# Attention scores masked in the accumulator bank, probabilities transposed before they are split, in a fused attention and two-layer MLP kernel

## The chip, the cores and the metric

One core of a Trainium2 chip runs the kernel. The metric is the device time of one execution in microseconds (us): the median of three runs, 1299.41 us (1298.48 to 1299.56) before the change. The engines are TensorE (PE; PEld for its weight loads), VectorE (DVE), ScalarE (ACT), GpSimd (POOL) and SyncE (SP, which issues the DMAs).

## The reference

The inputs are q, k and v of 4 batches, 8 heads, 768 positions and head size 64, in float32. Each query sees the first 4 keys (the sinks) and the last 128 keys up to itself; then come two dense layers over 3072 tokens.

```python
scores = scale * np.matmul(q, k.transpose(0, 1, 3, 2))
keep = is_sink | in_window
scores = np.where(keep, scores, -1000000000.0)
scores = scores - np.max(scores, axis=-1, keepdims=True)
a = np.exp(scores)
a = a / (np.sum(a, axis=-1, keepdims=True) + 1e-09)
x = np.matmul(a, v)                  # 3072 x 512 after the heads are joined
h = np.maximum(x @ moe_w_in, 0.0);  x = h * h @ moe_w_out         # 512 -> 2048 -> 512
h = x @ moe2_w_in;  out = (h - np.tanh(h)) @ moe2_w_out           # 512 -> 2048 -> 512
```

## The kernel before

**Precision.** Most matmuls take float32r operands (a reduced float32 that TensorE takes at full rate). To keep float32 accuracy an operand is split in two: `xh` is the value rounded to float32r, `xl` the rest. A product is then three matmuls (high by high, low by high, high by low). The first 16 jobs of attention, the *plain* ones, use unsplit float32 instead.

**Attention.** A *job* is one head of one half sequence (384 queries); 64 jobs make 8 *blocks* of 384 tokens. Jobs 0 to 15 are plain (`plain`), jobs 16 to 63 are split (`job`, `scores`, `values`): 48 of them. A job has three *units* of 128 queries. A unit multiplies its queries with 260 key columns: the 128 keys before its own, 4 sink keys, its own 128 keys (lines 323 and 324, the high and the low part of the keys; one result bank `S` for all units). Then ACT or DVE copies 132 columns of `S` to the tile `cb` (line 332 and the copies before it, recorded as line 257 on ACT and 259 on DVE), DVE overwrites with the earlier keys where the mask `up` says so (line 332, `copy_predicated`: a query has 128 keys in its window, and every column holds either an earlier or an own key), DVE adds the mask `m` and takes the row minimum of the negated scores (`least`, line 393, a custom instruction followed by a read of its accumulator `nm`), and ACT takes the exponential and the sum (line 336). After three units the sums are inverted (340, 341) and `cb` is multiplied by them (349). The first unit of a sequence's first half has no earlier keys: its two parts are copied one by one, without line 332.

**Transposition.** The 384 probability columns of a job are split into the float32r tiles `a` (high: a cast of 384 columns, on ACT or DVE; low: a subtraction on DVE, recorded as line 267). TensorE transposes both into bank `T` in two groups: four transpositions for the first two units (line 368), then two for the third and one for the sinks' tile `ask` (370). Each group is copied out to `xe` (or `pt`), and POOL selects from `xe` the own and the earlier keys into `pt` (line 382). Lines 413 to 418 multiply the values with `pt` into bank `O`; DVE joins the parts (429, 431) and splits the result into `xh`, `xl`, the input of the first layer.

**Layers.** `step1` makes one of 16 hidden slices of the first layer for a block: 12 matmuls into bank `ph` (line 579), relu (609 on ACT, 611 on DVE), square (615, 617), split into `gh` and `gl`, and 12 matmuls into four `acc` banks (593). `step2` is the second layer with 512 columns (579, 595). Weights arrive as 64-bit words and are decoded and split by `w_split` (lines 552 to 565).

**What sets the order.** Every operation is entered with its reads, its writes, a priority (a due time in planned microseconds) and its assumed duration per engine. `Order.solve` plays the program through with these durations: at each point an engine takes the most urgent operation that is ready, and operations that can run on more than one engine go where they would end first. The instructions are then issued in that order, each engine's queue in order. A wrong assumed duration therefore changes no result, but makes an engine wait in front of an instruction that came too early in its queue.

Of the kernel before, what the change touches and what calls it, by code (L numbers as in the profile page):

```python
# [33 lines left out]
KW = (3 * P + 2 * SK, 4 * P + 3 * SK)  # L34
# [28 lines left out]
class Op:  # L63
    __slots__ = ("engs", "prio", "emit", "left", "out", "ready", "start", "eng", "end")
# [13 lines left out]
class Order:  # L78
# [11 lines left out]
    NEAR = 60.0  # L90

# [3 lines left out]
    def add(self, engs, prio, reads, writes, emit):  # L95
        op = Op()
        op.engs, op.prio, op.emit, op.left, op.out, op.ready, op.eng = engs, prio, emit, 0, [], {}, None
        deps = set()
        for k in reads:
            if k in self.writer:  # L100
                deps.add(self.writer[k])
            self.readers.setdefault(k, []).append(op)
        for k in writes:
            if k in self.writer:
                deps.add(self.writer[k])
            deps.update(self.readers.pop(k, ()))
            self.writer[k] = op
        deps.discard(op)
        for d in deps:
            d.out.append(op)  # L110
        op.left = len(deps)
        self.ops.append(op)
# [3 lines left out]

    def solve(self):
        free = {e: self.AHEAD.get(e, 0.0) for op in self.ops for e in op.engs}
        avail, pend = {e: [] for e in free}, {e: [] for e in free}
        rank = {id(op): i for i, op in enumerate(self.ops)}  # L120
# [3 lines left out]
        def offer(op):  # L124
            for e in op.engs:
                heapq.heappush(pend[e], (op.ready.get(e, 0.0), rank[id(op)], op))

        for op in self.ops:
# [6 lines left out]
        def cost(op, e, now):  # L135
            c = op.engs[e]
            if e == "T":
                n = int((self.FIRST + now) // self.TICK)
                t = c[0] if tick.get(n - 1, 0.0) >= 0.375 * self.TICK else 2.0 * c[0]
                tick[n] = tick.get(n, 0.0) + c[0]  # L140
                return t, t + c[1] - c[0]
            return c[0], c[1]

# [4 lines left out]
        while len(done) < n:  # L148
            e = min(free, key=lambda g: free[g])
            now = free[e]  # L150
# [4 lines left out]
            best, held, skipped = None, None, []  # L155
            while avail[e]:
# [5 lines left out]
                if all(max(free[g], op.ready.get(g, 0.0), port if op.engs[g][2] else 0.0) + queue(g, item) + op.engs[g][1] >= at + op.engs[e][1]  # L162
                       for g in op.engs if g != e):
                    if at <= now + self.NEAR:
                        if held is None or now + op.engs[e][0] <= held[0] + self.NEAR:
                            best = op
                            break
                    elif held is None:
                        held = (at, item)
                        continue  # L170
                skipped.append(item)
            if held is not None:
                if best is None:
                    best = held[1][2]
                else:
                    skipped.append(held[1])
            for item in skipped:
                heapq.heappush(avail[e], item)
            if best is None:
# [4 lines left out]
                continue  # L184
            at = begin(best, e, now)
            occ, took = cost(best, e, at)
# [34 lines left out]
def c_copy(n, psum=False):  # L221
    return {"A": c_act(n, psum), "V": c_one(n, psum)}


def c_pool(n):
    return C(2.35 * n + 110, 2.35 * n + 115, True)
# [12 lines left out]
class Fast:  # L239
# [11 lines left out]
    def copy(self, prio, reads, writes, get, n, psum=False):  # L251
# [8 lines left out]
        self.o.add(c_copy(n, psum), prio, reads, writes, emit)  # L260
# [19 lines left out]
    def job(self, j, due):  # L280
# [24 lines left out]
        self.copy(d - 8, [("rv", r)], [("vh", k2)], lambda: (t["vv", k2][:, :nv, vh], vals()), nv * D)  # L305
# [4 lines left out]
    def scores(self, j, half, due):  # L310
# [4 lines left out]
        cb, nm, ss, rs, a, ask, xe, pt = ("cb", k2), ("nm", k2), ("ss", k2), ("rs", k2), ("a", 0), ("ask", k2), ("xe", 0), ("pt", 0)  # L315
        cbs = [(*cb, i) for i in range(3)]
        for i in range(3):
            d, ks = due[i], cbs[i:i + 1]
            col = 132 * i if half else 132 * max(i - 1, 0)

            def qk(e, i=i, col=col):
# [3 lines left out]
            o.add({"T": c_mm(260, 260)}, d - 14, [("qh", k2), ("ql", k2), ("kh", k2), ("kl", k2)], [sb], qk)  # L325
            if i < i0:
                self.copy(d - 13, [sb], ks, lambda i=i: (t[cb][:, i, :SK], bank[sb][:, 128:132]), SK, True)
                self.copy(d - 13, [sb], ks, lambda i=i: (t[cb][:, i, SK:], bank[sb][:, :128]), P, True)
            else:
# [4 lines left out]
            self.least(d - 11, ks[0], [(*nm, i)], lambda i=i: t[cb][:, i, :], lambda i=i: t[nm][:, i:i + 1], half, i, -0.125)  # L334
# [20 lines left out]
        self.copy(d - 8.9, cbs, [(*ask, 0)], lambda: (sinks(0), t[cb][:, :, :SK]), 3 * SK)  # L355
# [5 lines left out]
        def slots(i, n, s):  # L361
            return t[pt].rearrange("p (n t) q -> p n t q", t=2)[:, 2 * i:2 * (i + n), s, :]
        for u, n in ((0, 2), (2, 1)):
# [704 lines left out]
```

## Time and profile before

The profiled execution took 1298.54 us, of which the span from first to last instruction is 1296.8 us; the median of the runs is 1299.41 us.

| engine | busy us | share of span |
|---|---|---|
| PE | 1263.2 | 97% |
| DVE | 1054.7 | 81% |
| ACT | 674.6 | 52% |
| POOL | 184.7 | 14% |

The program has four stages, which overlap at their ends: plain attention and decoding of the first weights (to about 190 us); split attention beside the first layer (190 to 670); the end of the first layer beside the decoding of the second layer's weights (670 to 838); the second layer alone. In the rows below a stretch's line gives the length of the stretch, then per engine the busy time and the number of instructions, PE's granted clock (1.00 is 2.4 GHz), the DMA share and GB/s. A timeline line gives start, length, engine, line, operation and its tiles; matmuls overlap, so the time that one costs is the distance from its start to the next start. A line of instruction groups gives the count, busy time and mean ns of one, then the engine's idle time before them and who ended it. A line of waits gives total, times and longest.

### The profile page before, as it was taken

To read this page: it belongs to the slowest core of one execution; us is meant where nothing else is said; L and a number is where in the kernel's file an instruction comes from. 1 tells how busy PE (TensorE), PEld (TensorE's weight loads), DVE (VectorE), ACT (ScalarE), POOL (GpSimd) and SP (SyncE) were. 2 spreads that over 40 slices of the span, in tenths; PEclk is the share of its full clock that TensorE was granted. 3 is DMA by queue.
4 is the path that set the end of the run, shared out by engine and by line. 5 is a ranking of instruction groups with operands and counts; after the bars stand their busy time and mean duration, and the time that the engine had idled before them with its cause. 6 is when DMAs were issued, how large, how long until landed. Compare 5 with 4: busy or idle time off the path is not lost.

```text
span 1296.8 us, 19460 instructions
## 1 busy us (share of the span) xinstructions
PE 1263.2 (97%) x6696; PEld 1115.6 (86%) x6696; DVE 1054.7 (81%) x2550; ACT 674.6 (52%) x1723; POOL 184.7 (14%) x332
## 2 busy tenths in 40 slices
PE   8999999999999999999999999999999999999997
PEld 5789999999999999999999978888888888888886
DVE  6899998877878777878768999977877877877775
ACT  5776776655666556566545566433432433432332
POOL 1221343132112222112311200000000000000000
PEclk9999999999999999999999999999999999999999
DMA  6974112211212112122118830100100200000001
GB/s 214 320 260 153 45 56 77 83 54 44 80 45 84 58 46 75 53 60 83 29 34 286 280 107 1 33 33 1 63 3 1 66 1 1 33 1 1 33 1 35
DMA packets 41724, 95.00 MB, mean 73 GB/s; under 512 B 4752, under 2 KB 18576, under 8 KB 41616
## 3 DMA queue, kind: packets, MB, share of 16 engines
q1 hardware_dynamic: 41472, 93.27, 22.4%
q8 instruction: 54, 0.88, 0.3%
q10 hardware_dynamic: 144, 0.40, 0.1%
q14 instruction: 54, 0.44, 0.1%
HBM read 79.50 MB, written 14.16 MB: 72 GB/s over the span
## 4 chain that ended last, share of the span: by engine, by line
PE 75%; DVE 16%; ACT 4%; issue 3%; DMA 1%; POOL 1%; SPq 0%; DVEq 0%; ACTq 0%; POOLq 0%
PE ph L579 22%; PE acc L595 21%; PE acc L593 12%; PE S L579 10%; PE O L416 2%; PE T L368 2%; PE O L523 1%; PE S L323 1%; DVE xl L267 1%; DVE cb L332 1%; DVE x L429 1%; DVE qq L267 1%; DVE gl L267 1%; PE S L461 1%; DMA raw<-yd 1%
## 5 line engine op out<-in xcount | busy, mean ns | idle before, releaser
L579 PE MATMUL ph<-xh,w 128*128 128x384 f32 x1024 | 337.9, 342 | 2.9 <-ACT r L609 2.6
L593 PE MATMUL acc<-gh,w 128*128 128x384 f32 x1024 | 315.2, 342 | 0.0
L595 PE MATMUL acc<-w,g2h 128*128 128x512 f32 x768 | 301.6, 396 | 1.0 <-DVE g2h L259 1.0
L579 PEld LDWEIGHTS ph<-xh,w 128*128 128x128 f32 x1024 | 191.2, 188 | 6.2 <-ACT r L609 5.2
L593 PEld LDWEIGHTS acc<-gh,w 128*128 128x128 f32 x1024 | 189.5, 188 | 1.2 <-ACT y L257 0.5
L595 PEld LDWEIGHTS acc<-w,g2h 128*128 128x128 f32 x768 | 144.5, 188 | 36.0 <-DVE g2h L259 1.5
L593 PE MATMUL acc<-gl,w 128*128 128x384 f32 x512 | 173.8, 339 | 1.1 <-DVE gl L267 1.1
L579 PE MATMUL ph<-xl,w 128*128 128x384 f32 x512 | 171.7, 335 | 0.0
L595 PE MATMUL acc<-w,g2l 128*128 128x512 f32 x384 | 152.7, 398 | 0.2 <-DVE g2l L267 0.2
L579 PE MATMUL ph<-x2h,w 128*128 128x512 f32 x384 | 150.2, 394 | 2.7 <-DVE w L646 2.7
L579 PE MATMUL S<-x2h,w 128*128 128x512 f32 x384 | 149.4, 390 | 0.0
L382 POOL TENSOR_SCALAR_AFFINE_SELECT pt<-xe 128x256 fp32r<-128x256 f32 (+1 forms) x192 | 93.6, 514 | 135.5 <-DVE xe L259 84.7
L635 ACT ACTIVATE u<-ph 128x512 f32<-128x512 f32 x48 | 28.7, 597 | 157.3 <-PE ph L579 157.3
L642 DVE TENSOR_SCALAR mk<-u 128x512 uint8<-128x512 f32 x96 | 41.5, 432 | 74.6 <-ACT u L635 74.6
L593 PEld LDWEIGHTS acc<-gl,w 128*128 128x128 f32 x512 | 96.3, 188 | 5.0 <-DVE gl L267 4.5
L267 DVE TENSOR_TENSOR gl<-r,gh 128x384 fp32r<-128x384 f32 x123 | 69.3, 564 | 36.6 <-ACT gh L257 35.9
L579 PEld LDWEIGHTS ph<-xl,w 128*128 128x128 f32 x512 | 96.4, 188 | 0.4
L635 ACT ACTIVATE u<-S 128x512 f32<-128x512 f32 x48 | 28.7, 598 | 130.4 <-PE S L579 130.1
L336 ACT ACTIVATE cb<-cb,nm 128x132 f32<-128x132 f32 x144 | 58.4, 406 | 66.6 <-DVE nm L393 65.3
L579 PEld LDWEIGHTS ph<-x2h,w 128*128 128x128 f32 x384 | 72.9, 190 | 19.8 <-DVE w L646 3.0
L579 PEld LDWEIGHTS S<-x2h,w 128*128 128x128 f32 x384 | 72.2, 188 | 16.5
L595 PEld LDWEIGHTS acc<-w,g2l 128*128 128x128 f32 x384 | 71.8, 187 | 16.6 <-DVE g2l L267 0.5
(187 smaller groups left out, 2509.5 us busy)
## 6 DMA issues: line engine op xcount, KB each, us to landing
wr<-w SPq DMA_DIRECT2D x64, 512.0 KB, 5.6
raw<-raw SPq DMA_DIRECT2D x32, 454.0 KB, 3.4
raw<-raw SPq DMA_DIRECT2D x31, 388.0 KB, 3.1
yd<-y SPq DMA_DIRECT2D x40, 192.0 KB, 1.9
raw<-yd SPq DMA_DIRECT2D x28, 256.0 KB, 3.0
out<-y SPq DMA_DIRECT2D x20, 256.0 KB, 2.0
raw<-raw SPq DMA_DIRECT2D x24, 160.0 KB, 2.3
raw<-raw SPq DMA_DIRECT2D x24, 128.0 KB, 2.2
```

What stands on the lines that cost most here:

```text
L267: (nc.vector if e == "V" else nc.gpsimd).tensor_tensor(out=out, in0=a, in1=b.bitcast(F32), op=ALU.subtract)
L323: nc.tensor.matmul(out=bank[sb][:, :260], lhsT=lhs, rhs=kh[:, col:col + 260], start=True, stop=False)
L332: lambda e, i=i: nc.vector.copy_predicated(out=t[cb][:, i, SK:], mask=self.c["up"][:, 0, :], data=bank[sb][:, :128]))
L336: lambda e, i=i: nc.scalar.activation(out=t[cb][:, i, :], in_=t[cb][:, i, :], func=AF.Exp, bias=t[nm][:, i:i + 1], scale=-1.0, accum_out=t ...
L368: nc.tensor.transpose(out=tt[:, (2 * i + l) * P:(2 * i + l + 1) * P], in_=t[a][:, l, u + i, :], identity=self.c["id"])
L382: lambda e, u=u, n=n, s=s, sign=sign, op=op: nc.gpsimd.affine_select(out=slots(u, n, s), in_=t[xe][:, 2 * u:2 * (u + n), :], pattern=[[0, ...
L416: nc.tensor.matmul(out=oo[:, c:c + cnt * P], lhsT=vv[:, b - 2, :], rhs=pt[:, k + 2 * l:k + 2 * l + 3 * cnt - 2:3, :], start=(n == 0 and l ...
L579: nc.tensor.matmul(out=ph[:, :N], lhsT=w[:, a + c * P:a + (c + 1) * P], rhs=b[:, c, :], start=(c == 0 and k == 0), stop=(c == NE - 1 and k ...
L593: nc.tensor.matmul(out=acc[:, :N1], lhsT=w[:, a + e_ * P:a + (e_ + 1) * P], rhs=g, start=st, stop=sp)
L595: nc.tensor.matmul(out=acc, lhsT=g[:, e_ * P:(e_ + 1) * P], rhs=w[:, a:a + 512], start=st, stop=sp)
L635: o.add({"A": c_act(N2, True)}, v + 1.5, [pb], [u], lambda e: nc.scalar.activation(out=T[u], in_=self.bank[pb], func=AF.Square))
L642: lambda e: nc.vector.tensor_scalar(out=T[mk], in0=T[u], scalar1=U_MAX, scalar2=None, op0=ALU.is_lt))
```

## The change

- `scores` and `plain`: the copy of the scores out of the bank is gone. `copy_predicated` now writes in place in the bank (columns 132 to 259), and `least` reads the bank and writes `cb`. The bank is thus released by `least` instead of by `copy_predicated`.
- A first unit of a first half multiplies with 132 key columns (4 sinks, 128 own keys) instead of 260; the host puts the sinks ahead of the first keys (`layout`), and the mask `m0` and a loop over sink products in `plain` follow that.
- The tile `a` is gone. `cb` itself is transposed, in float32, by three transpositions, with the sinks' float32r transposition behind them in the same group; the high part is a cast of 384 columns out of bank `T` (ACT or DVE), the low part a subtraction on DVE that reads bank `T`; POOL then selects in two instructions of up to 768 columns instead of four.
- The scheduler: PE prefers an operation that has been ready for 250 ns in its own reckoning (`SAFE`); a few assumed durations change (`c_pool`, copies with `apart`, `least` without the shared port). `clocked` is the former `cost` moved.

```diff
-KW = (3 * P + 2 * SK, 4 * P + 3 * SK)
+KW = (3 * P + 3 * SK, 4 * P + 3 * SK)
...
+    SAFE = {"T": 250.0}
...
                         if held is None or now + op.engs[e][0] <= held[0] + self.NEAR:
-                            best = op
-                            break
+                            if op.ready.get(e, 0.0) + safe <= now:
+                                best = item
+                                break
+                            close = close or item
...
-    return C(2.35 * n + 110, 2.35 * n + 115, True)
+    return C(max(2.35 * n + 110, 290.0), None, True)
...
-                nc.tensor.matmul(out=bank[sb][:, :260], lhsT=lhs, rhs=kh[:, col:col + 260], start=True, stop=False)
-                nc.tensor.matmul(out=bank[sb][:, :260], lhsT=lhs, rhs=kl[:, col:col + 260], start=False, stop=True)
+                nc.tensor.matmul(out=bank[sb][:, :n], lhsT=lhs, rhs=kh[:, col:col + n], start=True, stop=False)
+                nc.tensor.matmul(out=bank[sb][:, :n], lhsT=lhs, rhs=kl[:, col:col + n], start=False, stop=True)
...
-                self.copy(d - 13, [sb], ks, lambda i=i: (t[cb][:, i, :], bank[sb][:, 128:260]), 132, True)
-                o.add({"V": c_two(P, True)}, d - 12, [sb] + ks, ks,
-                      lambda e, i=i: nc.vector.copy_predicated(out=t[cb][:, i, SK:], mask=self.c["up"][:, 0, :], data=bank[sb][:, :128]))
...
+            if i >= i0:
+                o.add({"V": c_two(P, True)}, d - 12, [sb], [sb],
+                      lambda e: nc.vector.copy_predicated(out=bank[sb][:, 132:260], mask=self.c["up"][:, 0, :], data=bank[sb][:, :128]))
+
+            self.least(d - 11, [sb], [ks[0], (*nm, i)], lambda n=n: bank[sb][:, n - 132:n], lambda i=i: t[cb][:, i, :],
+                       lambda i=i: t[nm][:, i:i + 1], half, i, -0.125)
...
-        self.copy(d - 9, cbs, [(*a, 0)], lambda: (t[a][:, 0], t[cb][:, :, SK:]), N1)
-        self.sub(d - 8, cbs + [(*a, 0)], [(*a, 1)], lambda: (t[a][:, 1], t[cb][:, :, SK:], t[a][:, 0]), N1)
...
+        def tr(e):
+            for i in range(3):
+                nc.tensor.transpose(out=bank[tb][:, i * P:(i + 1) * P], in_=t[cb][:, i, SK:], identity=self.c["idf"])
+            nc.tensor.transpose(out=bank[tb].bitcast(F32R)[0:96, 3 * P:], in_=t[ask], identity=self.c["id"])
+        o.add({"T": C(3 * 110.0 + 62.0, 560.0)}, d - 7, cbs + [(*ask, 0), (*ask, 1)], [tb], tr)
...
+        self.copy(d - 6, [tb], [(*xe, 0)], lambda: (halves(0), part()), N1, True)
+        o.add({"V": c_two(N1, True)}, d - 5.5, [tb, (*xe, 0)], [(*xe, 1)],
+              lambda e: nc.vector.tensor_tensor(out=halves(1), in0=part(), in1=halves(0).bitcast(F32), op=ALU.subtract))
...
+    def keys(half, i):
+
+        return (132 * i, 260) if half else (132 * i - 128, 260) if i else (0, 132)
...
-            for i in range(i0, 3):
+            for i in range(3):
                 nc.tensor.matmul(out=out[:, i * P:(i + 1) * P], lhsT=v[0:96, (i - 1) % 3, :], rhs=t[ps][0:96, :], start=False, stop=(i == 2))
...
-    for half, ks, vs_ in ((0, [kb[0], sk, kb[1], sk, kb[2]], range(3)), (1, [kb[2], sk, kb[3], sk, kb[4], sk, kb[5]], range(2, 6))):
+    for half, ks, vs_ in ((0, [sk, kb[0], sk, kb[1], sk, kb[2]], range(3)), (1, [kb[2], sk, kb[3], sk, kb[4], sk, kb[5]], range(2, 6))):
```

PE's queue at the transpositions of a split job, beside the first layer (names carry buffer numbers; `ph` and `acc` are the layer's matmuls). Before, two groups with nine layer matmuls between them:

```order
L368 MATMUL T_61<-idr,a_1259 128x128 x4
L579 MATMUL ph_450<-xh_182,w_2_0_694 128x384
L579 MATMUL ph_450<-xl_184,w_2_0_694 128x384
L579 MATMUL ph_450<-xh_182,w_2_0_694 128x384
L593 MATMUL acc_446<-gh_171,w_1_1_732 128x384
L593 MATMUL acc_446<-gl_173,w_1_1_732 128x384
L593 MATMUL acc_446<-gh_171,w_1_1_732 128x384
L579 MATMUL ph_450<-xh_182,w_2_0_694 128x384
L579 MATMUL ph_450<-xl_184,w_2_0_694 128x384
L579 MATMUL ph_450<-xh_182,w_2_0_694 128x384
L368 MATMUL T_61<-idr,a_1259 128x128 x2
L370 MATMUL T_61<-idr,ask_1261 96x128
```

Each group takes its own turn of the bank `T`. After, in the same part of the program, one group, here straight behind another job's scores:

```order
L324 MATMUL S_463<-kh_1232,qq_1230 128x260
L325 MATMUL S_463<-kl_1234,qq_1230 128x260
L358 MATMUL T_61<-idr,cb_1237 128x128 x3
L359 MATMUL T_61<-idr,ask_1245 96x128
L576 MATMUL ph_462<-xh_181,w_4_0_722 128x384
```

Seven transpositions in two places became four in one place.

DVE's queue between a unit's scores and its minimum, same part of the program. Before, the bank `S` is free after line 332:

```order
L259 COPY cb_1251<-S_451 128x132
L267 TENSOR_TENSOR vv_1250<-raw,vv_1250 128x5x64
L429 TENSOR_TENSOR x_1267<-O_62,tmp_1266 64x384
L332 COPY_PREDICATED cb_1251<-up,S_451 128x128
L431 TENSOR_TENSOR x_1267<-x_1267,tmp_1266 64x128
L393 ISA cb_1251,nm_1253<-cb_1251,m_77 128x132
```

The minimum (the last row) works on `cb` and holds up no bank. After, the bank is free after line 390:

```order
L426 TENSOR_TENSOR x_1252<-O_62,tmp_1251 64x384
L329 COPY_PREDICATED S_463<-up,S_463 128x128
L428 TENSOR_TENSOR x_1252<-x_1252,tmp_1251 64x128
L268 TENSOR_TENSOR ask_1246<-cb_1238,ask_1246 128x3x4
L390 ISA cb_1237,nm_1239<-S_463,m_77 128x132
L390 ISA nm_1239 128x1
```

The copy has left the queue, and instructions that stood behind the bank's release now stand ahead of it (here two).

## Rows read from the trace of the kernel before

**Rows 1.** The page, busy time by engine.

```profile
PE 1263.2 (97%) x6696; PEld 1115.6 (86%) x6696; DVE 1054.7 (81%) x2550; ACT 674.6 (52%) x1723; POOL 184.7 (14%) x332
```

**Rows 2.** Stretches: busy us of PE, PEld, DVE, ACT, POOL by stage.

```profile
30.00:190.00 160.00, 155.20 (x914) 140.03 (x913) 151.19 (x406) 115.94 (x332) 50.47 (x66) 1.00 0.50 168
190.00:670.00 480.00, 468.90 (x2937) 451.55 (x2938) 377.19 (x1179) 291.23 (x876) 116.26 (x237) 1.00 0.21 62
670.00:838.00 168.00, 163.28 (x801) 144.11 (x800) 153.33 (x280) 93.81 (x171) 12.51 (x11) 0.99 0.40 132
838.00:1258.00 420.00, 420.00 (x1810) 339.61 (x1809) 329.88 (x542) 146.46 (x260) 0.00 (x0) 1.00 0.06 20
```

**Rows 3.** Waits of PE: us in total, times, longest.

```profile
PE S L323 <- DVE cb L332: 5.9, 20, 0.5
PE T L368 <- DVE a L267: 4.2, 10, 0.5
```

**Rows 4.** Timeline of PE, split job: transpositions, then scores.

```profile
413.90 0.46 PE L368 MATMUL T<-idr,a 128*128 128x128 f32 x4
414.20 0.41 PE L593 MATMUL acc<-gh,w 128*128 128x384 f32 x1
414.44 0.34 PE L593 MATMUL acc<-gl,w 128*128 128x384 f32 x1
...
415.32 0.29 PE L368 MATMUL T<-idr,a 128*128 128x128 f32 x2
415.44 0.23 PE L370 MATMUL T<-idr,ask 128*96 128x128 f32 x1
415.52 0.41 PE L593 MATMUL acc<-gh,w 128*128 128x384 f32 x1
415.76 0.34 PE L593 MATMUL acc<-gl,w 128*128 128x384 f32 x1
...
416.11 0.29 PE L323 MATMUL S<-kh,qq 128*128 128x260 f32 x1
416.24 0.28 PE L324 MATMUL S<-kl,qq 128*128 128x260 f32 x1
416.36 0.33 PE L579 MATMUL ph<-xh,w 128*128 128x384 f32 x1
```

**Rows 5.** Timeline of PE, plain job: float32 transpositions among layer matmuls.

```profile
60.33 0.49 PE L502 MATMUL T<-idr,pcb 128*128 128x128 f32 x3
60.66 0.27 PE L503 MATMUL T<-idr,psk 128*96 128x128 f32 x1
60.69 0.42 PE L579 MATMUL ph<-xh,w 128*128 128x384 f32 x1
60.95 0.33 PE L579 MATMUL ph<-xl,w 128*128 128x384 f32 x1
61.12 0.51 PE L579 MATMUL ph<-xh,w 128*128 128x384 f32 x2
```

**Rows 6.** Groups of DVE, 0 to 754 us, shapes apart.

```profile
L393 DVE CUSTOM_DVE_ANT_0 cb<-cb,m 128x132 f32<-128x132 f32 x144 | 44.6, 310 | 3.3 <-ACT cb L257 1.1
L332 DVE COPY_PREDICATED cb<-up,S 128x128 f32<-128x128 uint8 x120 | 35.4, 295 | 3.6 <-ACT cb L257 2.2
L267 DVE TENSOR_TENSOR a<-cb,a 128x384 fp32r<-128x384 f32 x48 | 26.5, 551 | 0.6 <-ACT a L257 0.4
L429 DVE TENSOR_TENSOR x<-O,tmp 64x384 f32<-64x384 f32 x48 | 26.4, 551 | 2.6 <-ACT tmp L257 1.9
L259 DVE CAST a<-cb 128x384 fp32r<-128x384 f32 x33 | 18.1, 547 | 0.4
L259 DVE CAST gh<-r 128x384 fp32r<-128x384 f32 x49 | 17.6, 359 | 3.7 <-ACT r L615 3.7
L393 DVE DVE_READ_ACCUMULATOR2_ANT nm<- 128x1 f32 x144 | 11.6, 80 | 0.0
```

**Rows 7.** Group of ACT, 0 to 754 us: the copy of the scores.

```profile
L257 ACT COPY cb<-S 128x132 f32<-128x132 f32 x92 | 24.2, 263 | 21.7 <-PE S L324 21.3
```

More of the change, by code (lines that the diff above doesn't have):

```diff
@@ L63 @@
 class Op:
-    __slots__ = ("engs", "prio", "emit", "left", "out", "ready", "start", "eng", "end")
+    __slots__ = ("engs", "prio", "emit", "left", "deps", "out", "rank", "ready", "start", "eng", "end")
 class C(tuple):
@@ L125, in offer @@
             for e in op.engs:
-                heapq.heappush(pend[e], (op.ready.get(e, 0.0), rank[id(op)], op))
+                heapq.heappush(pend[e], (op.ready.get(e, 0.0), op.rank, op))
+        for op in self.ops:
+            op.left, op.ready, op.eng = len(op.deps), {}, None
         for op in self.ops:
@@ L149, in solve @@
             e = min(free, key=lambda g: free[g])
-            now = free[e]
+            now, safe = free[e], self.SAFE.get(e, 0.0)
             while pend[e] and pend[e][0][0] <= now:
@@ L385, in scores @@
-        for i in range(3):
-            self.copy(d - 6, [tb], [("pts", k2, i)], lambda i=i: (t["pts", k2][0:8, i * P:(i + 1) * P], bank[tb][32 * i:32 * i + 8, 2 * P:3 * P]), P, True)
-    def least(self, prio, cb, out, get, nm, half, i, scale):
+        def tr(e):
+            for i in range(3):
+                nc.tensor.transpose(out=bank[tb][:, i * P:(i + 1) * P], in_=t[cb][:, i, SK:], identity=self.c["idf"])
+            nc.tensor.transpose(out=bank[tb].bitcast(F32R)[0:96, 3 * P:], in_=t[ask], identity=self.c["id"])
@@ new lines, in scores @@
+        for s, sign, op in ((1, 1, ALU.is_ge), (0, -1, ALU.is_gt)):
+            u = 0 if s else i0
+            o.add({"P": c_sel(2 * P * (3 - u))}, d - 5, [(*xe, 0), (*xe, 1)], [("pt", 2 * i + s) for i in range(u, 3)],
+                  lambda e, u=u, s=s, sign=sign, op=op: nc.gpsimd.affine_select(
+                      out=t[pt].rearrange("p (n t) q -> p n t q", t=2)[:, 2 * u:, s, :], in_=t[xe][:, 2 * u:, :].bitcast(F32),
+                      pattern=[[0, 2 * (3 - u)], [sign, P]], compare_op=op, fill=0.0, base=0, channel_multiplier=-sign))
@@ L457, in plain @@
             sb = [("wide", m2, i)] if wide else [("S", 0)]
[L458 to L469 removed]
+            col, n = self.keys(half, i)
@@ new lines, in plain @@
+            o.add({"T": c_mm(n, n, slow=1.85)}, due[i] - 14, [("rq", q), ("rk", q)], sb,
+                  lambda e, i=i, col=N1 + col, n=n: nc.tensor.matmul(out=place(i)[:, :n], lhsT=t["raw", q][:, i * P:(i + 1) * P],
+                                                                     rhs=t["raw", q][:, col:col + n], start=True, stop=True))
+            if i >= i0 and not wide:
+                o.add({"V": c_two(P, True)}, due[i] - 12, sb, sb,
+                      lambda e, i=i: nc.vector.copy_predicated(out=place(i)[:, 132:260], mask=self.c["up"][:, 0, :], data=place(i)[:, :128]))
@@ L470, in plain @@
+            if not wide:
+                self.least(due[i] - 11, sb, [cbs[i], (*nm, i)], lambda i=i, n=n: place(i)[:, n - 132:n], lambda i=i: t[cb][:, i, :],
+                           lambda i=i: t[nm][:, i:i + 1], half, i, -0.0625)
         if wide:
-            sb, n = [("wide", m2, i) for i in range(i0, 3)], 3 - i0
-            self.copy(d - 13, sb, cbs[i0:], lambda: (t[cb][:, i0:, :], bank["wide", m2][:, i0:, 128:260]), 132 * n, True)
-            o.add({"V": c_two(P * n, True)}, d - 12, sb + cbs[i0:], cbs[i0:],
-                  lambda e: nc.vector.copy_predicated(out=t[cb][:, i0:, SK:], mask=self.c["up"][:, i0:, :], data=bank["wide", m2][:, i0:, :128]))
+            sb = [("wide", m2, i) for i in range(i0, 3)]
@@ L475, in plain @@
+            o.add({"V": c_two(P * (3 - i0), True)}, d - 12, sb, sb,
+                  lambda e: nc.vector.copy_predicated(out=bank["wide", m2][:, i0:, 132:260], mask=self.c["up"][:, i0:, :], data=bank["wide", m2][:, i0:, :128]))
         for i in range(3):
-            ks = cbs[i:i + 1]
-            self.least(due[i] - 11, ks[0], [(*nm, i)], lambda i=i: t[cb][:, i, :], lambda i=i: t[nm][:, i:i + 1], half, i, -0.0625)
+            ks, n = cbs[i:i + 1], self.keys(half, i)[1]
+            if wide:
+                self.least(due[i] - 11, [("wide", m2, i)], [cbs[i], (*nm, i)], lambda i=i, n=n: place(i)[:, n - 132:n], lambda i=i: t[cb][:, i, :],
+                           lambda i=i: t[nm][:, i:i + 1], half, i, -0.0625)
@@ L830, in prepare @@
         nc.scalar.activation(out=c["sqb"], in_=c["sqb"], func=AF.Copy)
-        v.memset(m0[:, :SK], -BIG)
         v.memset(lim, 0.0)
```

128 lines of the change are left out of this document (45 added, 83 removed).

## The prediction

> **What bounds the kernel now.** I read the busy times of the page first: PE works in 97% of the span, DVE in 81%, ACT in 52% [rows 1]. Then the stretches, because that mean hides four stages with different limits [rows 2]. From 838 us the second layer has PE busy in all of its 420 us; nothing in the change can shorten that. From 190 to 670 us, where most of the 48 split jobs run beside the first layer, PE is busy 468.9 of 480 us and DVE 377.2: PE is the bound, and its list of work is fixed, so a microsecond of PE work less is nearly a microsecond of time less. The 11.1 us in which it is seen idle there are what a better order could still give. From 30 to 190 us DVE is busy 151.2 of 160 us and PE 155.2: either may be late, so savings on one of them count for little. From 670 to 838 us it is alike (153.3 and 163.3 of 168), with no attention left.
>
> Next I asked the waits for what PE stands still [rows 3]. Two of its waits belong to the code that changes: scores wait for the bank `S` until line 332 has read it (5.9 us, 20 times), transpositions wait for the low half of `a` (4.2 us, 10 times). Last came the timeline of PE, to price its work: matmuls overlap, so a mean duration is no price, and the distance between starts is.
>
> **Transpositions (PE, 48 jobs).** Before: four start at 413.90 and the next matmul at 414.20, so 0.30 us; that matmul holds PE for 0.24 us, where a 384-column one otherwise takes 0.17 (60.95 to 61.12) [rows 4, 5], so 0.07 more goes to the group. The second group takes 0.20 (415.32 to 415.52) and again 0.07. In sum 0.64 us a job. After: one group of three float32 transpositions and the float32r one. Three float32 ones with their sinks took 0.36 in a plain job (60.33 to 60.69), and the matmul behind them 0.26, 0.09 more: 0.45 [rows 5]. The split job's sinks stay float32r and cost 0.08 (415.44 to 415.52) [rows 4] instead of 0.03: 0.33 + 0.08 + 0.09 = 0.50. The gain is 0.14 to 0.19 us a job; I take 0.14, since the sinks' own row is the nearer: 48 x 0.14 = **6.7 us**, with 9.1 at the other end.
>
> Here one rule speaks against the change. Rows 5 show 0.11 us for a 128-column float32 transposition, and rows 4 show 0.06 to 0.08 for a float32r one. The Trainium skill (FP8 and Floating Point Precision, section TensorE Precision Notes) says that true float32 takes four passes through the array. By that, three would take 3 x 4 x 0.06 = 0.72 us instead of 0.33 and the change would lose; rows 5 already disagree for transpositions, so the sum goes by the row, and the rule is a rival below.
>
> **Scores of first units (PE, 24 of the split jobs).** Two matmuls of 260 columns take 0.25 us (416.11 to 416.36). For two of 132 columns the nearest row is two transpositions of 128 columns: 0.12 (415.32 to 415.44), or 0.19 with the 0.07 behind them [rows 4]. So 24 x 0.06 to 0.13, 1.4 to 3.1 us; I take **2 us**. In the eight plain jobs of first halves the shorter scores and the added sink product are one to two units of 0.11 us each [rows 5], with opposite signs: nothing.
>
> **Waits for `a`.** The tile and its subtraction are gone, 0.55 us of DVE between the normalised probabilities and the transposition, and the cast (0.55) before it [rows 6]. The chain that feeds the transposition is now line 349, then a copy and a subtraction of 12 columns. The 4.2 us of waits [rows 3] go; what is late next is the sinks' tile, which in the order stands a few short DVE instructions behind line 349. I count **4 us**, and zero to six as bounds.
>
> **Waits for `S`.** The copy out of the bank goes: ACT did 92 of them in 24.2 us [rows 7]. Beside other work on an engine that is busy for 291 of 480 us [rows 2], its busy time is worth nothing by itself; it matters as a link. The bank was free after an ACT copy (0.26) and line 332 (0.30), and is now free after 332 and the minimum with its accumulator read (0.31 + 0.08) [rows 6, 7]: 0.56 us before and 0.69 after, one crossing between engines less. But both links stand in DVE's queue, and the order puts other instructions between them, two in the piece shown, 0.3 us and more. Behind a late minimum stand the next unit's scores on PE, and behind these the whole layer. The 5.9 us can so go to zero, or grow. I leave them at 5.9: **no change**, bounds from a gain of 6 to a loss of 12.
>
> **DVE and ACT.** Per split job DVE or ACT lose a cast of 384 columns, the copies of the scores and those of the transposed halves; DVE's subtraction of 384 columns stays, now out of a bank. No row shows DVE writing a bank. A lower bound is no difference (reading one costs nothing visible: 0.551 us with a bank as source and 0.551 without [rows 6]), and it might even be a little shorter; an upper bound is line 332 at twice its 0.295 us. I take no difference, the row with a bank as source being nearest. At the upper bound 120 units would hold `S` 0.3 us longer, which feeds the loss above. The scheduler spends what is freed: 94 casts `gh` instead of 49 now stand on DVE, 45 x 0.359 = 16 us [rows 6]. DVE is hidden behind PE from 190 us on; ahead of that it is not, and there I count **1 us** of gain for shorter chains, between a loss of 3 and a gain of 5. POOL issues half as many selections; with 185 of 1297 us [rows 1] they are hidden. No queue of SP is passed: the DMAs keep their places, and one is a few columns wider.
>
> A second rule: the row shows no cost of a bank as DVE's source at 384 columns. The Trainium skill (VectorE: DVE Perf Modes, section on the TRN2 errata) lists 120 cycles fixed for a PSUM source against 58 for an SBUF source; at its 0.96 GHz that is an estimate of 65 ns for each of 192 minima, 12 us of DVE in all, a quarter of it ahead of 190 us. By the rule the gain would be some 3 us smaller; by the rows, nothing.
>
> **The sum.** 6.7 + 2 + 4 + 0 + 1 = 13.7 us. The profiled execution took 1298.5 us, 1.7 more than its span and 0.9 less than the median of the three runs, so 1298.5 - 13.7 = 1284.8; I say 1285. If the likeliest case holds, 1279 to 1291.
>
> **Rivals.**
> 1. *The order gets better everywhere.* PE now prefers work that has been ready for a while, and most of its 11.1 us of idle time from 190 to 670 us could go, and 3 of 4.8 us before that. For it: the waits are short and repeat, as waits from wrongly assumed durations do [rows 3]. Against it: the waits for the layer's own operations are not touched. 1298.5 - 9 - 11 - 3 = 1275.
> 2. *The bank `S` becomes the bound (slower).* Place: PE in front of a unit's scores, line 390 as releaser. With the DVE queue full, each minimum comes late. For it: two DVE links in a row with other work between them, and DVE 79% busy in that stage [rows 2]. Against it: 48 split jobs in some 500 us are one every 10 us, 3 or 4 us for a unit, and the chain needs about 1.3 (0.28 for the last matmul, 0.69, and 0.3 between). The gain elsewhere is 13.7, so it decides from 0.10 us of added wait for each of 144 units; at 0.15 us the loss is 22 and the time 1298.5 + 8 = 1306.
> 3. *Nothing moves.* The gains on PE work are real, but new waits of some 9 us appear where the old ones went, at `nm`, `cb` or the single buffers `xe` and `T`, which one group now holds longer: 1298.5 - 13 + 12 = 1298, if the waits for `S` double and those for the transposition come back.
> 4. *Float32 transpositions cost four passes.* Place: PE, 48 groups. 0.72 + 0.08 + 0.09 = 0.89 us against 0.64 before is a loss of 12 us in place of the gain of 6.7: 1298.5 + 12 - 7 = 1304. Rows 5 speak against it. This is the rule of the Trainium skill named above.
>
> **How the numbers follow.** The forecast has 0.62, rival 1 0.13, rival 2 0.11, rival 3 0.12, rival 4 0.02. Two runs of this kernel differ by up to 0.1%, so 0.2% (2.6 us) is what can be told from no change. Faster by more than that holds in the forecast and rival 1 and, at its edge, in a third of rival 3: 0.79. Within: the rest of rival 3, 0.08. Slower: rivals 2 and 4, 0.13. The range takes in rival 1 and most of rival 3: 1272 to 1299, leaving out the 0.13 of the slow cases and a tail below.
>
> **What would show it.** Right, if after the change (a) a transposition group of three and one spans 0.4 to 0.45 us to the next start, with one slowed matmul behind it; (b) two 132-column scores take 0.12 to 0.19 us; (c) PE's waits have no line for `a`, and that for `S` now names the minimum, with about 6 us; (d) ACT is down by at least the 24 us of rows 7, with no effect of its own; (e) the second layer keeps its 420 us for five of six token blocks, and the whole gain lies before the second layer begins. Wrong, if the minimum reading the bank takes over 0.4 us, if the predicated copy into the bank takes twice its 0.295, or if PE's idle time ahead of the scores passes 20 us. If PE's work fell as worked out and the time did not, the order has put the waits elsewhere, and the sums of waits by releaser will name the place.

## The result: 1286.66 us, one per cent faster, by other terms than forecast

The changed kernel takes 1286.66 us (median of 4 runs, 1284.9 to 1288.81); in the same session the kernel before takes 1299.49 us (1298.48 to 1300.46). The ratio is 0.990, with a 95% interval of 0.9888 to 0.9913. The forecast was 1285. Its sum was right and several of its terms were not: the split stage gained more than forecast, a new chain of waits took part of it back, and the first stage lost where the forecast had it gain.

The profiled execution is the slowest of the four: 1288.81 us, with a span of 1286.8. The page's busy times and then the stretches, columns as in [rows 1, 2]; the last four lines are stretches of 5 us in the first stage:

```profile
PE 1255.7 (98%) x6568; PEld 1114.6 (87%) x6568; DVE 1031.0 (80%) x2488; ACT 630.8 (49%) x1493; POOL 152.3 (12%) x195
```

```profile
30.00:190.00 160.00, 150.74 (x862) 135.47 (x861) 147.02 (x402) 103.30 (x269) 35.41 (x45) 0.98 0.51 167
190.00:670.00 480.00, 474.56 (x2902) 462.42 (x2901) 357.96 (x1119) 266.57 (x735) 99.28 (x124) 1.00 0.21 63
838.00:1258.00 420.00, 420.00 (x1810) 339.87 (x1809) 328.46 (x540) 145.65 (x258) 0.00 (x0) 1.00 0.05 17
45.00:50.00 5.00, 2.71 (x15) 1.70 (x13) 4.60 (x16) 2.89 (x7) 0.19 (x1) 1.00 0.98 295
50.00:55.00 5.00, 3.76 (x11) 2.33 (x12) 5.00 (x15) 3.87 (x10) 1.70 (x2) 0.66 0.88 352
115.00:120.00 5.00, 2.49 (x14) 1.68 (x13) 4.94 (x12) 3.59 (x10) 0.93 (x1) 0.99 0.22 79
120.00:125.00 5.00, 5.00 (x23) 5.00 (x22) 3.74 (x9) 2.54 (x8) 0.00 (x0) 0.67 0.59 147
```

From 30 to 190 us PE is busy for 4.5 us less than before, and has done less by the end of it. Twice it stands still for half of 5 us, and in the 5 us behind its granted clock is 0.66 or 0.67, a mean of its two levels, 2.4 and 1.2 GHz. The kernel before has in the same stretches:

```profile
45.00:50.00 5.00, 4.87 (x30) 3.85 (x29) 4.13 (x16) 3.47 (x12) 1.31 (x2) 1.00 0.95 323
50.00:55.00 5.00, 4.43 (x26) 3.80 (x24) 4.29 (x14) 3.56 (x12) 1.19 (x2) 1.00 1.03 402
115.00:120.00 5.00, 5.00 (x30) 4.79 (x29) 4.97 (x13) 3.79 (x11) 1.11 (x1) 1.00 0.85 274
120.00:125.00 5.00, 5.00 (x32) 4.98 (x31) 5.00 (x14) 3.74 (x9) 0.00 (x0) 1.00 0.02 6
```

To see where time comes from, I compared when the same step of the first layer (128 of them) starts in both timelines. After is 8.8 us late at step 24 (196.1 us), still 5.2 late at step 48, level at step 64, 8.1 early at step 112 and 10.0 early from the second layer's step 8 to the end. So in this execution the first stage loses 9 us, the split stage gains 17, the passage into the second layer 2, and the second layer nothing.

PE's waits and, apart from them, those of its weight loads (columns as in [rows 3]; the first two lines of the weight loads before the change come third):

```profile
PE S L458 <- DVE pnm L390: 3.0, 2, 1.6
PE O L413 <- POOL pt L374: 1.8, 8, 0.3
PE ph L576 <- DVE xh L260: 1.4, 1, 1.4
```

```profile
PEld O L413 <- POOL pt L374: 8.7, 19, 0.6
PEld S L324 <- DVE nm L390: 3.3, 9, 0.4
```

```profile
PEld S L323 <- DVE cb L332: 12.5, 21, 0.8
PEld T L368 <- DVE a L267: 6.6, 12, 0.7
```

PE's lines for `S` of the split jobs and for `a` [rows 3] are gone. New is a wait of the values (`O`, line 413) for GpSimd's selection. Here a matmul that waits is first seen in its weight load: for the values PE's line has 1.8 us and the weight loads' line 8.7. What a wait costs is read from start to start: what lies between the start of the matmul ahead of a group and the start of the one behind it, beyond the usual distances. By that the values' waits cost 7.4 us from 190 to 670 us.

The timeline of PE, one transposition group and one first unit's scores, answering [rows 4]; then DVE's groups for [rows 6], 0 to 754 us:

```profile
508.27 0.49 PE L358 MATMUL T<-idr,cb 128*128 128x128 f32 x3
508.52 0.30 PE L359 MATMUL T<-idr,ask 128*96 128x128 f32 x1
508.66 0.39 PE L576 MATMUL ph<-xh,w 128*128 128x384 f32 x1
508.89 0.34 PE L576 MATMUL ph<-xl,w 128*128 128x384 f32 x1
...
313.41 0.22 PE L324 MATMUL S<-kh,qq 128*128 128x132 f32 x1
313.47 0.27 PE L325 MATMUL S<-kl,qq 128*128 128x132 f32 x1
313.58 0.39 PE L590 MATMUL acc<-gh,w 128*128 128x384 f32 x1
```

```profile
L390 DVE CUSTOM_DVE_ANT_0 cb<-S,m 128x132 f32<-128x132 f32 x144 | 41.5, 288 | 3.0 <-DVE S L329 0.5 <-PE S L325 0.5
L329 DVE COPY_PREDICATED S<-up,S 128x128 f32<-128x128 uint8 x120 | 34.6, 288 | 26.4 <-PE S L325 25.9
L370 DVE TENSOR_TENSOR xe<-T,xe 128x384 fp32r<-128x384 f32 x48 | 26.7, 557 | 15.4 <-ACT pts L258 15.2
```

A group takes 0.39 us (508.27 to 508.66) and slows one matmul from 0.17 to 0.23. The scores take 0.17 instead of 0.25. Reading and writing the bank costs DVE nothing that these rows show: the minimum takes 288 ns (310 before), the predicated copy 288 (295). The last line holds the surprise: in front of the subtraction DVE waited 15.2 us for ScalarE's copies of the *sinks*, which the subtraction does not use.

### The profile page after: what moved, and what is told of

Its sections match the earlier page's. It is cut to its first block, busy times and chain, and to the rows that moved or that the text cites. A ratio compares the mean times of both kernels' runs of the same rounds, so it can differ in the third digit from the quotient of the medians.

```text
span 1286.8 us, 18762 instructions
## 1 busy us (share of the span) xinstructions
PE 1255.7 (98%) x6568; PEld 1114.6 (87%) x6568; DVE 1031.0 (80%) x2488; ACT 630.8 (49%) x1493; POOL 152.3 (12%) x195
## 4 chain that ended last, share of the span: by engine, by line
PE 77%; DVE 10%; issue 5%; DMA 3%; POOL 2%; ACT 2%; DVEq 0%; SPq 0%; ACTq 0%; POOLq 0%
PE ph L576 23%; PE acc L592 21%; PE acc L590 12%; PE S L576 10%; POOL pt L374 2%; PE O L413 2%; PE O L520 2%; DMA yd<-y 1%; DVE wd L560 1%; PE T L358 1%; PE S L324 1%; DMA wr<-w 1%; PE S L325 1%; PE wide L458 1%; PE S L458 1%
## 5 line engine op out<-in xcount | busy, mean ns | idle before, releaser
L590 PE MATMUL acc<-gh,w 128*128 128x384 f32 x1024 | 322.4, 339 | 1.5 <-ACT y L258 1.4
L374 POOL TENSOR_SCALAR_AFFINE_SELECT pt<-xe 128x768 fp32r<-128x768 f32 x96 | 82.6, 885 | 346.5 <-DVE xe L370 346.5
L606 ACT ACTIVATE r<-ph 128x384 f32<-128x384 f32 x115 | 56.4, 491 | 57.0 <-PE ph L576 54.9
```

Of the source, the lines that this page charges most:

```text
L374: lambda e, u=u, s=s, sign=sign, op=op: nc.gpsimd.affine_select(out=t[pt].rearrange("p (n t) q -> p n t q", t=2)[:, 2 * u:, s, :], in_=t[x ...
L590: nc.tensor.matmul(out=acc[:, :N1], lhsT=w[:, a + e_ * P:a + (e_ + 1) * P], rhs=g, start=st, stop=sp)
L606: nc.scalar.activation(out=r, in_=ph, func=AF.Relu)
```

## The experiments

Ratios are to the kernel before on the same chip, with 95% intervals. "Steady" is the time from step 32 to step 104 of the first layer, with 36 split jobs: 401.1 us before, 386.0 after.

**e1: the transposition alone,** in the kernel before (`a` gone, one group, two selections; mask, scores and scheduler as before). Like e5 and e9 it drops from the values the sinks that lie ahead of a query in a sequence's first rows, which the reference counts (the expectation of e9 has this the other way round); its instructions are otherwise those of the change.

```diff
-        self.copy(d - 9, cbs, [(*a, 0)], ...)
-        self.sub(d - 8, cbs + [(*a, 0)], [(*a, 1)], ...)
...
+                nc.tensor.transpose(out=bank[tb][:, i * P:(i + 1) * P], in_=t[cb][:, i, SK:], identity=self.c["idf"])
```

Expected: 

> The kernel before with the new transposition alone (cb transposed in float32 in one group, split behind it); scores, scheduler rules and assumed durations as before. Theory A (the gain beside the first layer is the transposition: less PE work, and its waits for the low half gone): 48 x 0.14 to 0.19 us of PE work and 4 us of waits, so about 1288 us, with the wait for a gone from PE's list and the first stage unchanged within 2 us. Rival C (the gain is the scheduler's preference for work that is ready for long): the work alone, 1292 to 1293 us, with new waits in place of the old.

Measured: 1311.79 us, ratio 1.0099 (1.0083 to 1.0115): slower by 1%, and expected by neither theory. Step 32 starts 0.1 us later than before; steady is 412.1. The wait, and the stage:

```profile
PE O L410 <- POOL pt L376: 27.7, 41, 0.8
...
190.00:670.00 480.00, 452.11 (x2738) 433.17 (x2737) 363.79 (x1166) 278.79 (x785) 81.90 (x112) 1.00 0.21 63
```

In nearly every job the values wait: 27.7 us by PE's line, 38 from start to start. The timelines of ScalarE, DVE, GpSimd and PE for one job show the chain:

```profile
509.55 0.48 ACT L257 CAST xe<-T 128x384 fp32r<-128x384 f32 x1 [0.65 <-PE T L361]
...
510.06 0.57 DVE L259 CAST pts<-T 8x128 fp32r<-8x128 f32 x2
...
510.67 0.26 ACT L257 CAST pts<-T 8x128 fp32r<-8x128 f32 x1 [0.64 <-DVE pts L259]
...
511.02 0.56 DVE L372 TENSOR_TENSOR xe<-T,xe 128x384 fp32r<-128x384 f32 x1 [0.39 <-ACT pts L257]
...
511.66 1.45 POOL L376 TENSOR_SCALAR_AFFINE_SELECT pt<-xe 128x768 fp32r<-128x768 f32 x2 [2.68 <-DVE xe L372]
...
513.16 0.50 PE L410 MATMUL O<-pt,vv 128*128 128x256 f32 x2 [0.45 <-POOL pt L376]
```

Cast, copies and subtraction only read the bank `T`, yet they run one after the other, DVE's behind ScalarE's and ScalarE's behind DVE's, each released by a semaphore that the other engine raises. Below, these are called *turns*. From the cast's end to the subtraction's start the median is 1.00 us over 42 jobs. The scheduler does not reckon with that, and puts the values too early into PE's queue.

**e2: the mask alone** (mask in the bank, no copy out, 132-column scores, `layout`; transposition and scheduler as before).

```diff
-                self.copy(d - 13, [sb], ks, lambda i=i: (t[cb][:, i, :], bank[sb][:, 128:260]), 132, True)
...
+            self.least(d - 11, [sb], [ks[0], (*nm, i)], lambda n=n: bank[sb][:, n - 132:n], ...)
```

Expected: 

> The kernel before with the scores masked in the bank and the 132-column first units alone; transposition and scheduler as before. Theory A (the bank is held longer by the minimum, and in the first stage DVE puts weight decoding ahead of it): 2 us of PE work saved, 4 to 8 us lost before 190 us, so 1301 to 1306 us, with PE waiting for the minimum before 120 us. Rival B (the first stage is lost to the scheduler's new rules): no loss, 1295 to 1298 us.

Measured: 1284.59 us, ratio 0.9885 (0.9869 to 0.9902): as much as the whole change, where both theories had a smaller gain or a loss. Steady is 389.3 us. PE is busy 478.42 of 480 us and its own lines show no wait of note for `S` or `a`, but the weight loads' lines do for `a`:

```profile
PEld T L365 <- DVE a L267: 5.8, 19, 0.4
```

From start to start, 190 to 670 us, the waits for `S` fall from 9.8 to 1.4 us, and those for `a` only from 7.0 to 5.0. The mask removes the waits for `S`; most of those for `a` stay.

**e3: the scheduler alone** (margin and durations in the kernel before).

```diff
+    SAFE = {"T": 250.0}
...
-    return C(2.35 * n + 110, 2.35 * n + 115, True)
+    return C(max(2.35 * n + 110, 290.0), None, True)
```

Expected: 

> The kernel before with the scheduler's new rule (250 ns of readiness on PE) and assumed durations alone. Theory A: a few waits fewer, 1294 to 1299 us. Rival B: 5 to 8 us lost before 190 us, 1303 us or more if nothing is gained later. Rival C: most of the gain, 1288 us, with PE idle below 6 us from 190 to 670 us.

Measured: 1303.64 us, ratio 1.0036 (1.0022 to 1.0051). It is 8.8 us late at step 24 and 10.5 at step 32, regains 7 in the steady part (393.9), and ends 5 us late. The place is a wait of 3.8 us and a stretch behind it at the lower clock:

```profile
PE O L524 <- POOL ppp L517: 3.8, 1, 3.8
...
105.00:110.00 5.00, 2.35 (x14) 2.03 (x12) 5.00 (x11) 2.08 (x6) 4.47 (x1) 1.00 0.30 115
110.00:115.00 5.00, 3.83 (x15) 2.86 (x15) 0.27 (x1) 0.00 (x0) 2.13 (x6) 0.66 0.00 0
```

The scheduler's edit alone costs the first stage as much as the whole change does, at another place.

**e4: plain jobs as before,** in the changed kernel: their scores are copied out again.

```diff
+                self.copy(due[i] - 13, sb, cbs[i:i + 1], lambda i=i: (t[cb][:, i, :], place(i)[:, 128:260]), 132, True)
```

Expected: 

> The changed kernel, but the 16 plain jobs copy their scores out of the bank before masking, as they did before (132-column first units stay). Theory A: the waits of PE for the minimum at 46 to 52 us go, with them the half-rate stretch behind them; 4 to 6 us faster than the changed kernel, about 1281 us. Rival B: no difference, 1285 to 1288 us, since the first stage's loss lies elsewhere (at 115 us, in front of xh).

Measured: 1300.38 us, ratio 1.0002 (0.9992 to 1.0011). Both expectations missed. The theory that the plain jobs' waits for the minimum are the first stage's loss fell: it still loses 7.4 us by step 32. Worse, steady is 395.5, with split jobs whose code is that of the changed kernel; only the scheduler's order differs. Weight loads show more values waiting (8.7 us, 19 times, in the changed kernel); from start to start it is 12 us against 7:

```profile
PEld O L413 <- POOL pt L374: 14.1, 36, 0.7
```

**e5: e1 with a later priority for the copies of the sinks** (`d - 6` to `d - 5.4`).

Expected: 

> The transposition-only kernel (e1, 1311.8 us), with the three small copies of the sinks' rows out of bank T given a later priority than the subtraction, so that they stand behind it. As in e1 the first rows' sinks that lie ahead of a query are not counted. Theory D (in e1 the values' matmuls wait for POOL because the subtraction stands 1.0 us behind the cast, the small copies between them, which the scheduler does not reckon with): the subtraction follows the cast within 0.3 us, most of the 29 us of waits at V go, 1283 to 1295 us. Rival E (POOL's two selections of 0.86 us are what is late): the waits stay at half or more, 1300 us or more.

Measured: 1312.95 us, ratio 1.0091 (1.0074 to 1.0108), waits of 28.8 us: no effect, where the theory had 1283 to 1295. The rival (GpSimd's own selections are what is late) had 1300 or more; e9 below decides against it. From the cast's end to the subtraction's start it is still 1.00 us in the median: the later priority did not move the copies behind the subtraction.

**e6 and e7: the changed kernel without the margin, and with the old durations.**

```diff
-    SAFE = {"T": 250.0}
+    SAFE = {"T": 0.0}
```

Expected of e6: 

> The changed kernel with the scheduler's margin of 250 ns set to 0. Theory F (the margin is what keeps the values' matmuls from waiting for POOL): waits in front of the values' matmuls come back, 10 to 30 us of them, 1292 to 1312 us. Rival B (the margin is what costs the 8 us before 190 us): the first stage is 5 to 8 us shorter; both can be true, and then the time is near 1290.

Expected of e7: 

> The changed kernel with the old assumed durations of POOL subtractions and of copies beside other work; the margin of 250 ns stays. Rival B in its second form (the durations cost the first stage its 8 us): 1278 to 1281 us, step 24 of the first layer at 188 us and not at 196. If the margin costs it: 1285 to 1290 us and step 24 still near 196 us.

Measured: e6 1306.49 us, ratio 1.0042 (1.0025 to 1.0059); e7 1287.06, ratio 0.9896 (0.9879 to 0.9912). The durations do nothing measurable. Without the margin the change makes the kernel slower; the values' waits are back, 32 us from start to start:

```profile
PE O L413 <- POOL pt L374: 21.1, 39, 1.1
```

**e8: the three float32 transpositions issued twice,** in an order otherwise that of the changed kernel.

```diff
-            for i in range(3):
+            for i in (0, 1, 2, 0, 1, 2):
```

Expected: 

> The changed kernel, in the same order of instructions, with the three float32 transpositions of a job issued twice (same result): 48 x 0.33 us = 15.8 us more PE work, and PE's priority list is not told of it. If PE is the bound beside the first layer: 14 to 17 us longer, 1301 to 1304 us. If the waits are the bound, the added work falls into them: under 8 us longer.

Measured: 1299.18 us, ratio 0.9987 (0.9978 to 0.9997). The timeline of PE:

```profile
502.33 0.81 PE L358 MATMUL T<-idr,cb 128*128 128x128 f32 x6
502.91 0.30 PE L359 MATMUL T<-idr,ask 128*96 128x128 f32 x1
503.05 0.39 PE L576 MATMUL ph<-xh,w 128*128 128x384 f32 x1
```

A group takes 0.72 us instead of 0.39, so 48 x 0.33 = 15.8 us of PE work were added. The ratio rose by 0.0087, 11.3 us: some 70% of the work added to PE goes into the time. That is less than the 14 to 17 us expected of a pure bound by PE and more than the 8 us of the other theory: PE is most of the bound in this stage, and the rest fell into waits. A float32 transposition of 128 columns costs 0.11 us, not four times a float32r one (0.06 to 0.08 [rows 4]).

**e9, e10, e11: the turns taken away.** The three copies of the sinks now depend on the subtraction and so come behind it (e5 had the later priority without the dependency), in e9 in the kernel of e1, in e10 in the changed kernel, in e11 in the changed kernel without margin.

```diff
-            self.copy(d - 6, [tb], [("pts", k2, i)], ...)
+            self.copy(d - 5.4, [tb, (*xe, 1)], [("pts", k2, i)], ...)
```

Expected of e9: 

> The kernel of e1 (the changed transposition alone in the kernel before; like there, sinks that lie ahead of a query of the first rows are not masked out), but the three copies of the transposed sinks come behind the subtraction that makes the low half, no longer between the cast and it. Theory: ScalarE and VectorE take turns on the bank T, and the copies between cast and subtraction put the selection on GpSimd, and with it the values on PE, some 0.7 us later than the scheduler reckons. Then the cast's end to the subtraction's start falls from 1.0 to about 0.1 us, the 36 waits of some 0.8 us in front of the values all but go, and the time falls from 1312 to about 1288. Rival: the copies are innocent and the values are simply placed too early, by the missing margin: the waits stay at 25 us or more and the time at 1305 or more.

Expected of e10: 

> The changed kernel with the same edit: copies of the transposed sinks behind the subtraction. The values still wait 10 us in all for GpSimd there (25 times). Theory of the turns: these waits go, 1279 to 1284 us. Rival: with the margin the values already stand late enough in nearly all places, the waits left come from the order in the first stage: 1286 to 1289, no difference.

Expected of e11: 

> e10 without the margin of 250 ns. If the turns on the bank T are what the margin pays for, the 22 us of waits that e6 had do not come back, the first stage keeps part of the 8 us that the margin costs there, and the time is 1278 to 1288, against 1306 in e6. If the margin covers errors of the scheduler of every kind, the time stays near 1306.

Measured: e9 1272.55 us, ratio 0.9796 (0.9779 to 0.9812), 39 us under e1 with the same work. e10 1273.87, ratio 0.9803 (0.9785 to 0.982), better than both kernels. e11 1276.82, ratio 0.9826 (0.981 to 0.9843), 30 us under e6. All three came out below what was expected. What DVE's and the other engines' instructions on the tile `xe` waited for from 190 to 670 us (us, times), first in the changed kernel, then in e10:

```profile
its engine sat idle before it (us, times) until:
  DVE xe L370: 300.4, 44
  PE T L359: 19.6, 26
  ACT pts L258: 14.2, 38
```

```profile
its engine sat idle before it (us, times) until:
  DVE xe L370: 259.0, 44
  PE T L359: 10.4, 15
  ACT xe L258: 2.4, 10
```

The first line is GpSimd's own waiting for the subtraction. The copies (`pts`) are no longer among the releasers. The median from the cast's end to the subtraction's start is 0.98 us in the changed kernel, 0.03 in e9 and e11 and 0.40 in e10. No wait of the values for GpSimd is left in PE's lines in any of the three; from start to start it is at most 1 us, where e1 has 38, e6 32 and the changed kernel 7.4. The gains, 39, 30 and 13 us, go in the same order. e10's stages show what is left to gain:

```profile
30.00:190.00 160.00, 153.36 (x901) 139.35 (x900) 147.45 (x417) 106.33 (x275) 31.21 (x42) 1.00 0.51 168
190.00:670.00 480.00, 476.30 (x2952) 472.73 (x2951) 365.44 (x1127) 274.97 (x745) 96.83 (x125) 1.00 0.23 70
```

Its steady part takes 377.2 us (e9 380.2, e11 380.3). The margin, worth some 19 us in the changed kernel (e6), is worth 3 with the turns gone (e11): it was paying for them. e9 and e10 differ by no more than their intervals, so the mask, worth 15 us by itself, adds nothing measurable to e9. e11, which has the mask and not the margin, shows where it goes: its steady part is as long as e9's, and its step 32 starts 4.7 us later (in e10 4.1 later, with a steady part 3 us shorter). Part of the overlap is the waits for `S`: from start to start e9 has 4.7 us of them left without the mask, of 9.8 before. The rest of it is not traced.

**e12: e4 with the turns taken away.**

Expected: 

> e4 (the changed kernel with the plain jobs' scores copied out as before, 1300 us) with the edit of e9 and e10: the copies of the transposed sinks behind the subtraction. e4 had the same split jobs as the changed kernel and was still 14 us slower, with more values waiting for GpSimd. Theory: the turns on the bank T made it sensitive to where the scheduler happened to put the values, so without them both orders cost the same: 1270 to 1280, with no line of values waiting for GpSimd. Rival: the copies in the plain jobs themselves cost 14 us: 1285 to 1290, 14 more than e10.

Measured: 1284.23 us, ratio 0.9878 (0.9849 to 0.9908). 16 of e4's 26 us above e10 go, and with them all waits of values for GpSimd (12 us from start to start); that much was the turns. The other 10 stay, and grow through the split stage (1.7 us at step 32, 10.5 at step 112), where weight loads wait for the minimum; e10 has no such line:

```profile
PEld S L324 <- DVE nm L390: 6.6, 15, 0.6
```

Expected were 1270 to 1280: missed. That the plain jobs' copies cost it is not shown either, since the loss comes after them; the order of the split jobs differs, that wait explains 4 us from start to start, and what costs the rest stays open.

## Why the prediction was right, and where it was not

**Transpositions, 6.7 us.** The mechanism held and the size was too small: 0.39 + 0.06 = 0.45 us a job after, against 0.64, so 0.19 and 9.1 us, the other end of the sum. The sinks' transposition does not cost 0.08 on top: from the first start to the next matmul's it is 0.39 in all. Rival 4 fell (e8).

**First units' scores, 2 us.** Right: 0.08 x 24 = 1.9 [rows 4].

**Waits for `a`, 4 us.** They went, and were larger. In the timeline of before the first group of a job takes 0.297 us in the median and 0.455 in the mean over 44 jobs from 190 to 670 us, since its second transposition, that of a low half, sometimes waits: 0.158 x 44 = 7.0 us. The forecast read PE's line alone, 4.2 [rows 3]; the weight loads' line has 6.6.

**Waits for `S`, no change.** This step failed. From start to start they cost 9.8 us from 190 to 670 us; 2.5 are left after, so 7.3 went, in e2 by the mask alone. That lies beyond the forecast's bound of a gain of 6. The fear was other DVE instructions between two links of one queue. What the forecast gave too little weight is the link that left: the copy stood in another engine's queue or, 28 times of 120, in DVE's own; no run tests this reading by itself. Rival 2 fell: the minimum is no slower out of the bank, and the weight loads wait 3.3 us where they waited 12.5.

These four come to 9.1 + 1.9 + 7.0 + 7.3 = 25 us, and e10, without the turns, is 25.9 us faster than before. The terms that the forecast had are thus about the size of the gain that the change could bring; this is a match of sizes, not a run for each.

**What was missing.** The step "POOL issues half as many selections ... they are hidden" priced instructions and not the chain: cast, subtraction, two selections and then the values. With the turns on `T` inside it, the chain is about 1 us longer than the scheduler knows; e1 pays 38 us for it, from start to start. Rival 3 had named new waits behind `xe` and `T`, as 9 to 12 us and less likely; rival 1 had named the margin as a gain. Both happened: the margin moves the values back and saves 19 us (e6) of what the new chain costs. The Trainium skill (PSUM — Partial Sum Buffer, section "PSUM bank collisions raise a hardware error") has the rule: the compiler back end's scheduler puts a dependency between any two instructions of different engines that touch one bank in the same 32 partitions, reads against reads included. The trace agrees, with the 0.98 us above, and seems to go beyond it: in e1's timeline ScalarE's copy is released by DVE's copies, though the three read different groups of 32 partitions. The forecast had no term for it.

**First stage, 1 us of gain within a loss of 3 and a gain of 5.** Wrong in sign and outside its bounds: 9 us lost in the profiled execution. Two stalls begin it, at 45 to 52 us (plain scores behind a minimum that stands late in DVE's queue, 3.0 us) and at 115 to 121 (1.4 us for `xh` and others), each with a stretch behind it at a mean clock of 0.66 or 0.67. That clock does not follow from the changed instructions alone: e10 has the same PE instructions in the same order up to 148 us and the same stalls, and keeps 1.00:

```profile
45.00:50.00 5.00, 2.55 (x14) 1.54 (x12) 4.60 (x15) 2.89 (x7) 0.35 (x1) 1.00 0.96 296
50.00:55.00 5.00, 3.92 (x22) 2.75 (x22) 4.97 (x15) 4.17 (x11) 1.54 (x2) 1.00 0.87 345
120.00:125.00 5.00, 5.00 (x31) 5.00 (x30) 4.73 (x11) 3.00 (x8) 0.00 (x0) 1.00 0.73 208
```

At step 14, ahead of the first difference in order, the changed kernel is 7.7 us late and e10 4.5, so some 3 us of the 9 are the lower clock; e8 keeps 1.00 there too and is 5.7 us late at step 24. The stalls follow both edits: by step 12 every kernel with the mask or the scheduler's edit is 3.6 to 7.6 us late (e2 4.7, e3 6.6), and e1, e5 and e9, with neither, at most 1.2. By step 32 it ranges from 1.0 (e10) over 4.6 (e6) to 10.5 (e3). So the rest of the loss belongs to the orders that the scheduler happens to find, and which rule would avoid it stays open.

**The sum.** By the spans of the profiled executions the changed kernel (1286.8) is 15.4 us behind e10 (1271.4): 7.7 of it lie ahead of step 32 (some 3 of them the lower clock), 8.8 in the steady part, and behind that it regains 1.1. Of the 8.8, 6.2 are the values' waits from start to start and 2.4 the waits for `S` that e10 does not have. By the medians the distance is 12.8 us: a gain of 25.9 less 12.8 is what was measured. The forecast had 12.7 of the one and none of the other: its total was right because two omissions cancelled, which is luck.

**The signs to look for.** (b) and (e) held as written, (a) but for 0.01 us (0.39); (d) ACT is down by 44 us; (c) held for `a`, while the wait for `S` did not stay at 6 us but went. The sums of waits by releaser, of the last sentence, named the place: the values behind GpSimd's selection.

## What to carry to other kernels

- When two engines read one accumulator bank, count their reads as a chain in program order, and put the read that others wait for first. Here one added dependency, which delays three tiny copies, is worth 13 us in the changed kernel and 39 in e1.
- Where an assumed-duration scheduler fills the queues, a safety margin that helps much points to a dependency that its model lacks: look for that before tuning the margin.
- Price a wait from start to start, and read the weight loads' waits beside PE's. Gains measured for two edits alone need not add (15 and 27 us alone, 26 together).

## What was not expected of the hardware

- In these programs ScalarE and VectorE take turns on one bank, by semaphores, even where both only read it: three short copies of sinks put 0.98 us between a cast and the subtraction that follows from it.
- A bank as source and destination costs VectorE nothing at these sizes: 288 ns for the minimum out of the bank against 310 before, 288 against 295 for the predicated copy that now writes it. The Trainium skill's rule that the prediction weighed second (VectorE: DVE Perf Modes, section on the TRN2 errata) is not borne out by these rows.
- Equal standstills of PE do not always bring the clock down. Three times, twice in the changed kernel and once in e3, 2.3 to 2.7 us without work in 5 us were followed by 5 us at a mean granted clock of 0.66 or 0.67, part of it at 1.2 GHz. e10, with the same instructions and the same stall at 45 to 50 us (2.45 us without work), stayed at 2.4 GHz, and so did e7 and e8. No run shows what decides.
